# Scratch rows regrouped by their reader, and each unit's write cut in four

## The chip, the cores and the metric

The kernel runs on one core of one Trainium2 chip. The metric is the device time of one execution in microseconds (us), lower is better. On the core work TensorE (PE, matrix products), VectorE (DVE), ScalarE (ACT), GpSimd (POOL) and SyncE (SP, which only issues transfers here), and 16 DMA engines that carry all transfers between the on-chip buffers and DRAM. One execution is recorded by the hardware profiler; what it left is called the profile here (a page of summaries) and the trace (every instruction and transfer).

## The reference

The input `x` has 2048 rows of 1024 numbers. Two filters, A and B, are applied to it in the frequency domain and their results are mixed by a gate per row:

```python
x = A_x
g = sigmoid((x * gate_w).sum(-1, keepdims=True))
X = rfft2(x)                                   # 2048 x 513, complex
a = irfft2(X * (A_w_r + 1j * A_w_i), s=(S, D))
b = irfft2(X * (B_w_r + 1j * B_w_i), s=(S, D))
return g * a + (1 - g) * b
```

All inputs and the output are bfloat16; B's own `x` is not used.

## The kernel before, in words

The transforms are done as matrix products with constant matrices. The columns split into two halves, `par` 0 (even frequencies) and `par` 1 (odd). The work on rows goes forward in two steps (`f1`, 64 x 32), the columns are transformed in between, and the way back has the same two steps. Its tokens are:

- `r`, `f`, `E`, `O` (`f1`): the first step along rows, from `x` into the tile `Y`.
- `F` (`f2`, L375), `G` (`f3`, L394): per unit, the columns' transform and the second step along rows. There are 8 units (`u` = 0 to 7) per half; each has two tiles of 128 rows (`tt`).
- `c` (`cmul`, L415), with `d` (`edge`) and `a` (`part`): the product with the filter weights, on DVE; `w` (`load_w`, L232) loads the weights of a unit.
- `i` (`i1`, L453): the first step back. It runs twice per unit, `r` = 0 and 1 (real and imaginary part); its result is copied out of PSUM by ACT or DVE (L278, L280) into a buffer `rl` that holds, per partition, two tiles `tt`, two filters `a`, two parts `r` and 256 columns. After `r` = 1 the buffer is **written to a scratch tensor `sc` in DRAM** (L461).
- `q` (`fetch`, L470): **reads the scratch back**, with rows spread differently over the partitions. `q par.g.v` reads, for `v` of 8, what the four units of group `g` (units 0 to 3 or 4 to 7) wrote; it fills every second partition of a tile of 128 partitions with 4 KB each. So two fetches, g = 0 and g = 1, fill one tile.
- `j` (`i2`, L483): the second step back along rows, from such a tile, with the gate worked into its matrix `EAB`. `k` (`i3`, L498) and `D` (`i3d`, L532, L520): the transform of the columns back. `s` (`fold`, L551), `t` (`last`, L565 to L582): sums and differences, and the write of the output.

The scratch is there because the two steps back need different rows side by side on the partitions; the trip through DRAM does the exchange.

What sets the order is a list written out by hand, `ORDER`: one token after another is built, and each engine carries out its own instructions in that order. All loads, scratch writes, fetches and nearly all output writes are issued by SP, one after another; if one has to wait, everything behind it on SP waits. The writes stand in the list where their unit ends (`i0.1`, `i2.1`, `i1.1`, `i3.1`, `i4.1`, ... `i14.1`, `i15.1`); the half `par` 1 has units 8 to 15 in these tokens. Its first three fetches (`q1.0.1`, `q1.0.0`, `q1.0.2`) and then `q1.1.0` and the rest come behind `i15.1`. `j1.0` to `j1.7` read them.

Buffers are handed out by fixed lists (`SLOTS`). `rl` has 4 buffers, which the units of a half, and later the output, take in turn: a unit may write its buffer only when the transfers that read it before have landed. The transfers share 8 semaphores in turn, so that an issue also waits until the eighth transfer before it has landed.

The scratch is one tensor per half. Unit `u` writes, for each of its four (`tt`, `a`), 128 rows of 1 KB, one from each partition. Partition `p` is 32 k + s, with k from 0 to 3 and s from 0 to 31, and the fetch for `v` takes s from 4 v to 4 v + 3.

Of the kernel before, what the change touches and what calls it, by code (L numbers as in the profile page):

```python
# [10 lines left out]
P = 128  # L11
# [3 lines left out]
NU = 8  # L15
N1 = 32
N2 = 64
BF16 = mybir.dt.bfloat16
# [139 lines left out]
def gated_mix(ctx, tc, x_in, we_in, wo_in, gw_in, out):  # L158
    nc = tc.nc
# [18 lines left out]
    def take(tag, *dims):  # L178

        t = slots[tag][int(next(order[tag]))][:, 0:int(np.prod(dims))]  # L180
        ax = "abcd"[:len(dims)]
        return t.rearrange(f"p ({' '.join(ax)}) -> p {' '.join(ax)}", **dict(zip(ax, dims)))

    def halves():
        return [bank(), bank()]
# [18 lines left out]
    XR = [big.tile([P, 2064], BF16, name=f"xr{v}") for v in range(8)]  # L204
    RO = [big.tile([P, 2064], BF16, name=f"ro{v}") for v in range(8)]
# [7 lines left out]
    Ec = const.tile([P, N2], BF16, name="ec")  # L213
    Ez = const.tile([64, N2], BF16, name="ez")
    scratch = ctx.enter_context(tc.tile_pool(name="scratch", bufs=1, space=bass.MemoryType.DRAM))
    sc = [scratch.tile([NU, 4, P, 512], BF16, name=f"sc{par}") for par in range(2)]
    Y = big.tile([P, 2, 2, 2, 16, 2, 32, 2], BF16, name="y")
    y = [Y[:, par] for par in range(2)]
    wod = [big.tile([P, 2048], BF16, name=f"wo{k}") for k in range(4)]
# [56 lines left out]
    def evac(eng, out, in_):  # L276
        if eng == "A":
            nc.scalar.copy(out=out, in_=in_)  # L278
        else:
            nc.vector.tensor_copy(out=out, in_=in_)  # L280
# [6 lines left out]
    def hp(j):  # L287
        return slice(64 * j, 64 * j + 64)
# [153 lines left out]
    def i1(n, r, eng="A"):  # L442
        par, u = n // NU, n % NU
        p = Ps[n]
        o = 1 if par == 0 and r == 1 else 0
        ps = halves()
        terms = (((0, 0, 0), (2, 0, 1), (3, 1, 1), (2, 1, 0)), ((1, 0, 0), (0, 0, 1), (2, 1, 1), (0, 1, 0)))[r]
        terms = [z for z in terms if z[1:] not in summed.get(n, ())]
        for k, (w, q, a) in enumerate(terms):
            for tt in range(2):  # L450
                for j in range(2):
                    hin = hp(j ^ tt)
                    nc.tensor.matmul(ps[tt][hp(j), :], lhsT=WI[hin, 2 * u + tt, w, :],  # L453
                                     rhs=p[hin, q, tt, a::2, o:o + 256], start=(k == 0), stop=(k == len(terms) - 1))
        if r == 0:
            RLs[n] = take("rl", 2, 2, 2, 256)
        rl = RLs[n]
        for tt in range(2):
            evac(eng[tt % len(eng)], rl[:, tt, :, r, :], ps[tt][:].rearrange("p (a m) -> p a m", a=2))
        if r == 1:  # L460
            nc.sync.dma_start(sc[par][u].rearrange("t p f -> p t f"), rl[:].rearrange("p t a r m -> p (t a) (r m)"))  # L461
            RLs.pop(n), Ps.pop(n)

    def rows(par, v):
# [1 line left out]

    def fetch(par, g, v):

        src = sc[par][4 * g:4 * g + 4].rearrange("u t (k s) f -> (u t k) (s f)", k=4)
        nc.sync.dma_start((XR, RO)[par][v][g::2, 0:2048], src[:, 2048 * v:2048 * v + 2048])  # L470

    Vs, EVs = {}, {}
    IGU = FD[:, 0].rearrange("p a b m -> p (a b m)").rearrange("p (c a d) -> p c a d", c=2, a=2)
# [113 lines left out]
    def run(tok):  # L587
        op, a, e = tok[0], tok[1:].split(":")[0], tok.split(":")[1] if ":" in tok else ""
        n = [int(q) for q in a.split(".")] if a else []
        if op in "rfEO":  # L590
            f1(((n[0], 0), (n[0], 1)) if op in "rf" else ((n[0], "EO".index(op)), (n[0] + 1, "EO".index(op))), e)
        elif op in "VQ":
            xfold(n[0], op)
        elif op == "h":
            gt["z"] = gate_hat()
        elif op == "l":
            late()
        else:
            dict(F=f2, G=f3, d=edge, c=cmul, i=i1, w=load_w, g=gate_z, q=fetch, j=i2, k=i3, D=i3d,
                 s=fold, a=part, t=last)[op](*n, *([e] if e else []))  # L600
# [57 lines left out]
```

## Time and profile before

| | |
|---|---|
| time, three runs | 112.97, 118.17, 167.16 us (median 118.17) |
| the profiled execution | 113.11 us, of which the span of the profile is 111.3 us |
| busy, share of the span | PE 89%, ACT 84%, DVE 83%, POOL 7% |
| scratch writes | 16 of 512 KB, median 6.0 us from issue to landing |
| fetches | 32 of 256 KB, median 5.2 us (`par` 0) and 5.5 us (`par` 1) |
| DMA | 37.07 MB, mean 333 GB/s, 18,594 packets |
| granted TensorE clock | 1.00 |

How to read it: the span runs from the first to the last instruction. The busy time of an engine is the time in which it carries out instructions; matmuls are pipelined and their ends are modelled. A wait is counted for the engine that stands idle, under the name of what ended it. "SPq" is SP's sequence of transfers, where the listed duration is that of the issue, not of the transfer. Landing is the moment when a transfer's semaphore is complete. The lines that the argument rests on are shown where it is made.

### The profile page before, as it was taken

To read this page: it belongs to the slowest core of one execution; us is meant where nothing else is said; L and a number is where in the kernel's file an instruction comes from. 1 tells how busy PE (TensorE), PEld (TensorE's weight loads), DVE (VectorE), ACT (ScalarE), POOL (GpSimd) and SP (SyncE) were. 2 spreads that over 40 slices of the span, in tenths; PEclk is the share of its full clock that TensorE was granted. 3 is DMA by queue.
4 is the path that set the end of the run, shared out by engine and by line. 5 is a ranking of instruction groups with operands and counts; after the bars stand their busy time and mean duration, and the time that the engine had idled before them with its cause. 6 is when DMAs were issued, how large, how long until landed. Compare 5 with 4: busy or idle time off the path is not lost. (4 is left out here: it accounts for less than half of the span.)

```text
span 111.3 us, 4030 instructions
## 1 busy us (share of the span) xinstructions
PE 99.1 (89%) x1656; PEld 68.5 (62%) x1656; DVE 92.3 (83%) x145; ACT 94.0 (84%) x185; POOL 7.4 (7%) x14
## 2 busy tenths in 40 slices
PE   5959989799999999999999999995999775999740
PEld 2339979475556658656765677654699564664430
DVE  0169957399899999999999999995989869699770
ACT  2246977599899999999999999999799798999740
POOL 1000000121592000000000000000000000000000
PEclk9999999999999999999999999999999999999999
DMA  3899999999999998995999999999995789998974
GB/s 106 223 361 415 405 397 406 414 411 388 412 397 409 398 333 262 367 392 181 260 359 334 363 316 386 362 317 378 322 276 217 224 228 358 399 408 358 366 281 128
DMA packets 18594, 37.07 MB, mean 333 GB/s; under 512 B 2188, under 2 KB 11024, under 8 KB 18576
## 3 DMA queue, kind: packets, MB, share of 16 engines
q1 hardware_dynamic: 17696, 36.37, 90.5%
q10 hardware_dynamic: 848, 0.45, 1.4%
q8 instruction: 13, 0.21, 0.7%
q14 instruction: 5, 0.04, 0.1%
q0 software_dynamic: 32, 0.00, 0.0%
HBM read 24.23 MB, written 12.58 MB: 331 GB/s over the span
## 5 line engine op out<-in xcount | busy, mean ns | idle before, releaser
L453 PE MATMUL pt<-p,wi 64*64 64x512 bf16 x488 | 30.6, 377 | 0.0
L278 ACT CAST rl<-pt 128x512 bf16<-128x512 f32 x47 | 28.6, 920 | 0.7 <-PE pt L453 0.7
L415 DVE TENSOR_TENSOR p<-X,ro 128x4096 bf16<-128x4096 bf16 x11 | 25.1, 2293 | 0.4 <-ACT V L344 0.3
L278 ACT CAST T<-pt 128x512 bf16<-128x512 f32 (+1 forms) x40 | 23.2, 721 | 1.6 <-PE pt L532 0.6
L453 PEld LDWEIGHTS <-wi 64*64 64x64 bf16 x488 | 16.1, 106 | 9.6 <-issue 1.5
L278 ACT CAST X<-pt 128x512 bf16<-128x512 f32 x27 | 17.5, 824 | 0.9 <-PE pt L394 0.9
L278 ACT CAST V<-pt 128x512 bf16<-128x512 f32 x28 | 16.3, 690 | 1.6 <-PE pt L483 1.5
L278 ACT CAST y<-pt 128x512 bf16<-128x512 f32 x21 | 11.2, 627 | 5.6 <-PE pt L321 4.1
L375 PE MATMUL pt<-fd,y 128*128 128x256 bf16 x128 | 15.9, 273 | 0.0
L375 PEld LDWEIGHTS <-y 128*128 128x128 bf16 x128 | 11.6, 98 | 4.3 <-issue 2.9
L280 DVE CAST rl<-pt 128x512 bf16<-128x512 f32 x17 | 11.2, 677 | 0.1
L394 PE MATMUL pt<-T,wf 64*64 64x512 bf16 (+2 forms) x192 | 10.5, 307 | 0.6 <-issue 0.6
L498 PE MATMUL pt<-ig,V 128*128 128x256 bf16 x88 | 10.8, 273 | 0.0
L574 DVE TENSOR_TENSOR rl<-wo,T 128x1024 bf16<-128x1024 bf16 (+1 forms) x18 | 9.2, 569 | 1.6 <-ACT T L278 1.2
L498 PEld LDWEIGHTS <-V 128*128 128x128 bf16 x88 | 8.2, 98 | 1.5 <-issue 0.4
L415 DVE TENSOR_TENSOR p<-X,wo 128x4096 bf16<-128x4096 bf16 x4 | 9.1, 2274 | 0.0
L280 DVE CAST y<-pt 128x512 bf16<-128x512 f32 x11 | 7.4, 686 | 2.1 <-PE pt L324 2.0
L278 ACT CAST p<-pt 128x512 bf16<-128x512 f32 x15 | 8.5, 604 | 0.3 <-PE pt L498 0.2
L394 PEld LDWEIGHTS <-wf 64*64 64x64 bf16 x192 | 5.6, 107 | 3.3 <-issue 1.2
L369 POOL TENSOR_SCALAR ro<-ro 128x8 bf16<-128x8 bf16 x7 | 5.8, 850 | 22.6 <-DMA ro<-in_we_dram 22.6
L483 PE MATMUL pt<-eab,ro 128*128 128x64 bf16 x128 | 5.0, 193 | 2.6 <-DMA ro<-sc 1.9
L483 PEld LDWEIGHTS <-ro 128*128 128x128 bf16 x128 | 4.5, 98 | 3.8 <-issue 2.5
(57 smaller groups left out, 107.7 us busy)
## 6 DMA issues: line engine op xcount, KB each, us to landing
sc<-rl SPq DMA_DIRECT2D x16, 512.0 KB, 6.0
xr<-sc SPq DMA_DIRECT2D x16, 256.0 KB, 5.2
ro<-sc SPq DMA_DIRECT2D x16, 256.0 KB, 5.5
ro<-in_we_dram SPq DMA_DIRECT2D x7, 516.0 KB, 8.4
xr<-in_x_dram SPq DMA_DIRECT2D x6, 512.0 KB, 8.4
out_dram<-rl SPq DMA_DIRECT2D x5, 512.0 KB, 4.3
wo<-in_wo_dram SPq DMA_DIRECT2D x4, 512.0 KB, 7.8
ro<-in_wo_dram SPq DMA_DIRECT2D x4, 512.0 KB, 6.7
```

The source lines that it names most:

```text
L278: nc.scalar.copy(out=out, in_=in_)
L280: nc.vector.tensor_copy(out=out, in_=in_)
L369: nc.gpsimd.tensor_scalar(Ws[n][:, :, :, 257:258], Ws[n][:, :, :, 256:257], -1.0, None, ALU.mult)
L375: nc.tensor.matmul(ps[tt][:, e * 256:e * 256 + 256], lhsT=y[par][:, c, e, t].rearrange("p b s k -> p (b s k)"), rhs=FD[:, par, c, e, :], s ...
L394: nc.tensor.matmul(ps[tt][ho, dst:dst + ln], lhsT=WF[hp(j), 2 * u + tt, w, :], rhs=T[hp(j), tt, src:src + ln], start=(k == 0), stop=(k == 2))
L415: nc.vector.tensor_tensor(po, xo, wo, ALU.mult)
L453: nc.tensor.matmul(ps[tt][hp(j), :], lhsT=WI[hin, 2 * u + tt, w, :], rhs=p[hin, q, tt, a::2, o:o + 256], start=(k == 0), stop=(k == len(te ...
L483: nc.tensor.matmul(ps[s][:, ch * 128 + h * 64:ch * 128 + h * 64 + 64], lhsT=R[:, k, ch * 128:ch * 128 + 128], rhs=EAB[:, 4 * v + k, :], st ...
L498: nc.tensor.matmul(po, lhsT=V[:, s, 2 * r + c, :], rhs=IG[:, par, 2 * r + c, :], start=(c == 0), stop=(c == 1))
L574: nc.vector.tensor_tensor(o4[:, k, h] if not isinstance(od, list) else o4[:, k.start, h], x, y_, op)
```

## The change

The scratch tensor of a half, which had the dimensions unit, four (`tt`, `a`) rows, partition, 512 numbers, gets the dimensions group, 32 quarters of the partitions, 16 (unit of the group, `tt`, `a`), 4 partitions, 512 numbers. The four partitions that one fetch reads together still lie side by side (4 KB), and now the 16 such pieces of a group's units do as well (64 KB); before, they lay 128 KB apart. [...] The fetch reads the same rows into the same partitions in the same order.

```diff
-    sc = [scratch.tile([NU, 4, P, 512], BF16, name=f"sc{par}") for par in range(2)]
+    sc = [scratch.tile([2, 32, 16, 4, 512], BF16, name=f"sc{par}") for par in range(2)]
@@ i1
         if r == 1:
-            nc.sync.dma_start(sc[par][u].rearrange("t p f -> p t f"), rl[:].rearrange("p t a r m -> p (t a) (r m)"))
+            for tt in range(2):
+                for a in range(2):
+                    nc.sync.dma_start(sc[par][u // 4, :, 4 * (u % 4) + 2 * tt + a], rl[:, tt, a].rearrange("p r m -> p (r m)"))
             RLs.pop(n), Ps.pop(n)
@@ fetch
-        src = sc[par][4 * g:4 * g + 4].rearrange("u t (k s) f -> (u t k) (s f)", k=4)
-        nc.sync.dma_start((XR, RO)[par][v][g::2, 0:2048], src[:, 2048 * v:2048 * v + 2048])
+        src = sc[par][g].rearrange("(k v) t s f -> t k v (s f)", k=4)
+        nc.sync.dma_start((XR, RO)[par][v][g::2, 0:2048], src[:, :, v])
```

## The prediction

> **What bounds the kernel now.** I read busy time by stretches first, since a share over the whole span mixes stages. Columns: stretch, length, busy time of PE, PE's weight loads, DVE, ACT, POOL (instructions in brackets), granted clock, busy share of the DMA engines, GB/s.
>
> ```profile
> 68.00:72.00 4.00, 3.99 (x80) 2.79 (x76) 4.00 (x5) 4.00 (x11) 0.00 (x0) 1.00 1.07 376
> 72.00:76.00 4.00, 3.02 (x62) 1.84 (x53) 3.97 (x4) 4.00 (x10) 0.00 (x0) 1.00 1.00 334
> 76.00:80.00 4.00, 3.67 (x56) 2.51 (x57) 2.67 (x4) 3.21 (x7) 0.00 (x0) 1.00 1.06 374
> 80.00:84.00 4.00, 4.00 (x86) 3.78 (x84) 3.56 (x9) 4.00 (x9) 0.00 (x0) 1.00 0.85 259
> 84.00:88.00 4.00, 3.81 (x47) 3.21 (x45) 3.66 (x7) 3.74 (x8) 0.00 (x0) 1.00 0.61 196
> 88.00:92.00 4.00, 2.81 (x48) 2.49 (x48) 2.98 (x7) 3.07 (x7) 0.00 (x0) 1.00 0.85 245
> 92.00:96.00 4.00, 2.79 (x55) 2.00 (x54) 3.97 (x9) 3.47 (x8) 0.00 (x0) 1.00 0.98 368
> ```
>
> From 30 to 72 us ACT and DVE are full: nothing done to the scratch pays there. From 72 on they have holes. ACT idles 0.79 + 0.26 + 0.93 + 0.53 us in the rows above and 0.74 in 100 to 104: **3.25 us is the most that faster scratch traffic can return**. The waits of 72 to 108 us (engine and line, for what, us in total, times, longest) say whose holes they are:
>
> ```profile
> PE pt L483 <- DMA ro<-sc: 1.9, 3, 0.6
> ...
> PEld L483 <- DMA xr<-sc: 1.4, 1, 1.4
> ```
>
> L483 is `i2`, the reader of the fetches. Fetch by fetch: q1.1.1 lands at 89.78 and j1.1 starts at 89.82, q1.1.2 92.66 and 92.69, q1.0.6 99.30 and 99.32. So the second half's fetches pace the kernel from 88 to 99 us, and they are paced by three things. One: they may only start when i15.1's write has landed (issued 80.16, landed 85.34; SP waits 2.6 us for it, below). Two: SP issues one per 0.64 us. Three: stalls. Undisturbed fetches land 0.63 us apart (92.03, 92.66, 93.27, 93.91, 94.55), 416 GB/s; three gaps are longer (1.36, 2.26, 1.14 us), 0.72 + 1.61 + 0.50 = 2.8 us of stall in all. The packet records agree: a 4 KB packet takes 159 ns, in this stretch up to 1,833.
>
> Then SP's own waits, 50 to 72 us, whole, and the first of 72 to 96:
>
> ```profile
> SPq L470 <- DMA sc<-rl: 3.6, 2, 2.4
> SPq L461 <- ACT rl L278: 2.1, 4, 1.0
> SPq L461 <- ACT T L278: 1.6, 2, 1.2
> SPq L461 <- ACT X L278: 1.4, 1, 1.4
> SPq L256 <- PE pt L453: 1.2, 1, 1.2
> SPq L470 <- PE pt L453: 0.5, 1, 0.5
> ...
> SPq L461 <- DVE rl L280: 4.4, 2, 3.7
> SPq L470 <- DMA sc<-rl: 2.6, 1, 2.6
> SPq L461 <- ACT rl L278: 2.2, 3, 1.5
> ```
>
> The first six add to 10.4 us; 2.4 of them end at 50.3, so in 50.3 to 72 SP has **8.0 us to spare**. This is what the change spends.
>
> **The change, part by part.** (a) *48 more issues on SP*, three for each of 16 units. Their price is the unknown that decides. The rows for issues, with min/median/max ns:
>
> ```profile
> L470 SPq DMA_DIRECT2D ro<-sc x8: 594/596/599, 85.9 to 90.4; - x8
> ...
> L208 SPq DMA_DIRECT2D xr<-in_x_dram x5: 389/424/432, 0.7 to 2.6; - x5
> ...
> L461 SPq DMA_DIRECT2D sc<-rl x5: 359/360/366, 72.0 to 80.2; - x5
> ```
>
> An issue after a pause costs 0.36; back to back, a load of 128 rows costs 0.43 and a fetch of 64 rows 0.60, each plus 0.04 between. That the fetch's 0.594 to 0.599 doesn't move while landings stall says that it is the issue's own cost. The one other transfer of 64 rows, `ez`, took 0.52 where loads of 128 rows took 0.33. So the ends for a second write are 0.48 and 0.70 us (the fetch's 0.64 and some for one more dimension). The new write has 128 rows in the buffer and 32 in DRAM; a side with fewer than 128 rows is what sets the dear rows apart, so I take the fetch's **0.64**. A unit then holds SP for 0.42 + 3 x 0.64 = 2.34 us instead of 0.42.
>
> Before 50 us SP mostly waits for data (its next write is issued up to 4 us after the last), and the engines are full: free, as long as no weight load queued behind a write becomes late; the nearest, w14, has some 15 us. In 50.3 to 72 six units are written: 18 x 0.64 = 11.5 us against 8.0, so SP reaches i12.1 at 75.5 instead of 72.0. Then i12, i11, i13 and i14 take 4 x 2.34 = 9.4, to 84.9; their data was ready by 76, so the waits of this stretch are all eaten. i15.1's fourth issue comes at 84.9 + 0.42 + 1.28 = 86.6.
>
> (b) *Landing.* The old write lands 5.2 to 6.5 us after its issue, behind queued data. Paced by issues, 128 KB per 0.64 us is 205 GB/s, half of what the engines move, so the queue drains; a 128 KB output at the end lands 1.9 us after its issue, a 256 KB one 2.2. I take 2.2: the last piece lands at 88.8 instead of 85.34. The fetch q1.1.0 now waits for sixteen pieces instead of four transfers; behind it on SP stand the other fetches and then all output writes, and `i2` on PE waits for them: 13 fetches start **3.5 us late**. Eight transfers are in flight at most (each issue waits for the semaphore of the eighth before it); with small pieces that is 1 MB, 5.1 us of issues, so it binds only where landings take longer than that.
>
> The Trainium skill, "DMA: Bandwidth & Descriptors", section "Issuing engines are not separate DMA queues", holds that the time to start a transfer is usually small beside the transfer. Here 128 KB at 416 GB/s is 0.31 us, under any issue in the trace; by the page's rule part (a) would cost nothing and the faster rival below would follow.
>
> (c) *The `rl` buffers.* A unit's buffer comes free when all its writes have landed, and it is close already: i8's write lands at 71.33 and i13.0 is evacuated into the same buffer from 71.41; i10's 73.12 and i14.0 73.32; i12's 78.53 and i15.0 78.70. Later issues with quicker landings leave these between 0 and 1.5 us later; where they come later, ACT and PE stop. I count 0, since this lies ahead of, and beside, the lateness of (b), and keep 1.5 for the range.
>
> (d) *Fetches.* Same number, bytes and 4 KB runs; sixteen neighbouring pieces of 4 KB are read together where each group of four rows lay 128 KB from the next. Bounds for the stalls: none of 2.8 us goes, or all. The writes get a wide pitch in turn (two 4 KB runs per engine, engines 128 KB apart), so I take half: 1.4. The issue may cost 0.05 more with one dimension more; over 13 fetches 0.6, kept for the range.
>
> (e) *First half's fetches.* j0.2 waits for q0.1.2 (issued 71.12, landed 76.28). 3.5 us late in issue, 2 us quicker in landing: 1.5 us late, and it is part of the same lateness, as i15.0 stands behind j0.2 on PE.
>
> **Sum.** The first late fetch is 3.5 late, the last 3.5 - 1.4 = 2.1. ACT has 0.93 + 0.53 + 0.74 = 2.2 us of holes behind 88 us; late work fills some of them, but j1.6 starts at its fetch's landing and has 9 us of work behind it. So the end moves by 2.1 to 3.5 less what is filled: I take +2.6. On the profiled execution's 113.11 us (span 111.3 and 1.8 around it) this is **115.7 us**. The three runs shown are 112.97, 118.17 and 167.16, median 118.17; the profile belongs to the lowest, and I forecast beside that one.
>
> **Rivals.**
> *Cheap issues and no stalls: faster.* At 0.48, 18 x 0.48 = 8.6 exceeds the 8.0 by 0.6; four units of 1.86 end at 80.0, i15.1 is on time, its last issue is at 81.5 and lands at 83.7, 1.6 us earlier than now; with the 2.8 us of stalls gone, fetches run 4 us ahead and ACT's holes bound the gain: 1.6 to 3.2, say 110.7. It decides at an issue of about 0.52. For it: loads of 128 rows; against it: every transfer with 64 rows.
> *The pieces collide: much slower.* At 0.70, SP is 4.6 late at i12.1; 4 x 2.52 = 10.1; last landing near 90.7, 5.4 late; no stall goes, since now the writes stride; less 1 us filled: 117.5. With (c) added, 119.
> *No relief in the fetches, issues between.* At 0.55, 9.9 - 8.0 = 1.9 late; four of 2.07 from 73.9 end at 82.2, the last piece lands at 85.9, 0.6 late; stalls stay: 113.7, no change. The trace knows stalls without scratch: the x loads' 4 KB packets near 4 us took up to 1,353 ns. The Trainium skill's same page, "Latency and other measured facts", gives a row pitch of 512 KiB 207 of 214 GB/s, so a quarter of that pitch should cost almost nothing and the layout gains almost nothing; the fetches' gaps here (2.8 us on some 8) are more than that rule allows.
> *It doesn't do what it says.* If the interleaved writes were taken as overlapping, each would wait for the one before, over 2 us each, 64 times: above 200 us. Fetches g=0 and g=1 into alternate partitions of one buffer don't wait for each other now, so I give it 0.03.
>
> **Chances.** Forecast 0.40 (its times 114.3 to 117, four fifths of them over 2%), much slower 0.18, no relief 0.17, faster 0.22, wrong ordering 0.03. Slower by over 2% (about what a measurement here tells from no change), above 115.4: 0.32 + 0.18 + 0.03 = 0.53. Within 2%: 0.08 + 0.17 + 0.03 of the faster case = 0.28. Faster: 0.19. The range takes in the faster rival's 110.7 and the much slower one's 119: 110.5 to 119.
>
> **What would show it.** Write issues behind a unit's first: 0.60 right, under 0.45 wrong. SP's waits for ACT and DVE between 50 and 80 us nearly gone. i15.1's last piece landing near 88.8. Stretch 88 to 92 emptier on ACT than 3.07. Fetch landings evenly 0.64 apart if the layout helps. I am wrong if issues are cheap, or if SP's lateness is absorbed because the queue's backlog, not SP, set the landings.

## The result, and the profile after

The changed kernel takes 129.33 us (median; 127.28 to 129.91), the kernel before in the same measurement 115.66 (112.97 to 167.16): **slower, ratio 1.133, 95% interval 1.101 to 1.166**. The ratios here and below leave disturbed runs out, so they can differ from the quotient of the medians; for e5 to e9 only medians are given, and the traces of e8, e10, e12 and e14 are of disturbed runs. The forecast was 115.7 with a range of 110.5 to 119: the sign was right, the size was far off. The profiled execution took 127.28 us (before 113.11), of which the span is 125.2 (111.3).

The page of the changed kernel: span, busy time by engine, PE's and the granted clock's rows of slices of 3.1 us, and the issues of scratch writes and second-half fetches (count, size, median us to landing).

```profile
span 125.2 us, 4122 instructions
...
PE 102.9 (82%) x1656; PEld 69.6 (56%) x1656; DVE 92.5 (74%) x145; ACT 94.4 (75%) x185; POOL 7.1 (6%) x14
...
PE   6969897999999999999992599509999079959750
...
PEclk9999999999999999999999679985999968999999
...
sc<-rl SPq DMA_DIRECT2D x64, 128.0 KB, 3.6
...
ro<-sc SPq DMA_DIRECT2D x16, 256.0 KB, 6.0
```

PE was busy 99.1 us before and idle for 12.2 (111.3 less 99.1). Now it is idle for 22.3 (125.2 less 102.9): 10.1 us more waiting. The other 3.8 us are the same matmuls at a lower granted clock. Together that is the 13.9 us. PE's row has three holes ahead of its end (digits 2, 0 and 0), and behind each the clock's row drops. Stretch by stretch, with the columns of the table in the prediction:

```profile
66.00:70.00 4.00, 0.56 (x6) 0.25 (x3) 2.55 (x2) 2.07 (x5) 0.00 (x0) 1.00 0.94 270
70.00:74.00 4.00, 3.61 (x52) 2.28 (x56) 0.69 (x1) 1.74 (x4) 0.00 (x0) 0.57 0.96 303
74.00:78.00 4.00, 4.00 (x84) 2.14 (x80) 3.59 (x3) 4.00 (x9) 0.00 (x0) 1.00 0.72 227
78.00:82.00 4.00, 2.07 (x44) 1.07 (x36) 3.31 (x4) 3.36 (x7) 0.00 (x0) 1.00 1.05 267
82.00:86.00 4.00, 1.80 (x21) 1.55 (x22) 0.69 (x1) 0.59 (x1) 0.00 (x0) 0.72 0.84 275
```

In the first row PE stands for 3.4 of 4 us; in the second it works at a clock of 0.57. The full engines of 68 to 72 us before (3.99, 4.00 and 4.00 on PE, DVE and ACT) are gone. What PE waited for, from the waits of 30 to 126 us (engine and line, for what, us in total, times, longest; `i2` is L485 now, the fetch L472, the write L463):

```profile
PE pt L485 <- DMA ro<-sc: 5.5, 3, 3.8
...
PE pt L485 <- DMA xr<-sc: 4.1, 1, 4.1
...
PE pt L485 <- DMA sc<-rl: 3.8, 1, 3.8
...
DVE rl L280 <- DMA sc<-rl: 0.3, 1, 0.3
```

The three long ones are one fetch each. q0.1.0 lands at 70.26 (before 65.23) and j0.0 starts at 70.29; q0.1.2 lands at 84.16 (76.28), j0.2 starts at 84.20; q1.1.0 lands at 100.67 (88.42), j1.0 starts at 100.70. The release of the first carries the name of a scratch write because that came last by the profile, but j0.0's start goes with its fetch's landing. The fourth line is all that the `rl` buffers cost here by being held for scratch writes: 0.3 us.

From the landing of q1.1.0 to the end of the span the kernel takes 24.5 us (125.2 less 100.67), before 22.9 (111.3 less 88.42). So 12.2 of the 13.9 us are the lateness of this one landing, and what has to be explained is why it is so late.

Why the fetches are late is in SP's own sequence (start, length, what, count), of before and then of after:

```profile
72.00 8.53 SPq L461 DMA_DIRECT2D sc<-rl  x5
80.62 13.93 SPq L470 DMA_DIRECT2D ro<-sc  x16
```

```profile
75.77 3.14 SPq L472 DMA_DIRECT2D xr<-sc  x5
79.01 15.32 SPq L463 DMA_DIRECT2D sc<-rl  x20
94.37 10.84 SPq L472 DMA_DIRECT2D ro<-sc  x16
```

SP reaches i12.1 at 79.01 instead of 72.00 (forecast 75.5), and the twenty writes of the last five units hold it until 94.33. i15.1's last piece is issued at 93.73 and lands at 95.86 (forecast 86.6 and 88.8; before 80.16 and 85.34). The price of a write was forecast well. The issue rows of after (min/median/max ns), the writes and the fetches, from 60 and 96 us on:

```profile
L463 SPq DMA_DIRECT2D sc<-rl x34: 518/594/2102, 60.1 to 93.7; - x34
...
L472 SPq DMA_DIRECT2D ro<-sc x11: 514/593/595, 96.4 to 102.7; - x11
```

0.594 and 0.04 between: the 0.64 that was taken. But the first write of a unit costs it too (0.52 to 0.60, where 0.36 was read off the old write), so a unit holds SP for 2.55 us, not 2.34.

SP's sequence can be summed up. From i5.1's first write at 51.2 us to i15.1's last stand 44 writes, 15 fetches and a load, 60 issues. At 0.64 us from one start to the next, the last would start at **88.9 if SP never waited again** (51.17 + 59 x 0.64). The forecast's 86.6 was such a sum without waits too, with 0.42 us for the first write of each of the eleven units; the right price of these adds 2.3 us. Another 4.8 us came on the way to 93.73. The profile lists 6.2 us of waits for SP in 50 to 97 us, and these lead:

```profile
SPq L463 <- ACT rl L278: 1.8, 4, 0.5
SPq L463 <- ACT T L278: 1.0, 2, 0.5
SPq L463 <- ACT X L278: 0.7, 2, 0.6
```

They are short (0.6 us at most), and most of them end inside the issue that carries them: i7.1's first write, listed with a wait of 0.5 us, takes 0.556 us, and a piece without a wait 0.60. So they hardly lengthen the sequence, and SP's waits were nearly all eaten, as forecast. What lengthens it are five issues of 0.85 to 2.10 us (at 51.75, 58.87, 72.86, 79.62 and 90.94), 3.6 us beyond 0.60 each, and about 1.2 us of gaps for data and for landings; the other 55 issues take 0.51 to 0.62 us. For four of the five the profile names no wait. In the trace each of the five overlaps a load of 16 KB of instructions (packets of queue q8, from 51.33, 58.59, 72.47, 79.59 and 91.01 us; the last took 1.6 us, the issue beside it 2.1). In e3 the five longest issues of this stretch (at 51.79, 59.29, 72.54, 81.18 and 92.62) overlap such loads as well. That the loads make the issues long is suggested by this and not shown; in the kernel before, one of 1.14 us (at 56.87) has neither a wait nor a load beside it.

### The profile page after: what moved, and what is told of

It reads as the page before. It is cut to its first block, busy times and chain, and to the rows that moved or that the text cites. A ratio compares the mean times of both kernels' runs of the same rounds, so it can differ in the third digit from the quotient of the medians.

```text
span 125.2 us, 4122 instructions
## 1 busy us (share of the span) xinstructions
PE 102.9 (82%) x1656; PEld 69.6 (56%) x1656; DVE 92.5 (74%) x145; ACT 94.4 (75%) x185; POOL 7.1 (6%) x14
## 5 line engine op out<-in xcount | busy, mean ns | idle before, releaser
L278 ACT CAST rl<-pt 128x512 bf16<-128x512 f32 x47 | 27.3, 778 | 2.1 <-PE pt L453 2.1
L278 ACT CAST V<-pt 128x512 bf16<-128x512 f32 x28 | 15.0, 618 | 11.8 <-PE pt L485 11.8
L453 PEld LDWEIGHTS <-wi 64*64 64x64 bf16 x488 | 15.2, 108 | 10.9 <-issue 2.4
L278 ACT CAST X<-pt 128x512 bf16<-128x512 f32 x27 | 16.0, 763 | 1.6 <-PE pt L394 1.6
L500 PE MATMUL pt<-ig,V 128*128 128x256 bf16 x88 | 12.4, 299 | 0.0
L485 PE MATMUL pt<-eab,xr 128*128 128x64 bf16 x128 | 5.5, 205 | 8.0 <-DMA xr<-sc 4.1
L485 PE MATMUL pt<-eab,ro 128*128 128x64 bf16 x128 | 5.7, 205 | 5.5 <-DMA ro<-sc 5.5
L500 PEld LDWEIGHTS <-V 128*128 128x128 bf16 x88 | 9.0, 107 | 2.2 <-issue 0.4
L485 PEld LDWEIGHTS <-xr 128*128 128x128 bf16 x128 | 5.0, 105 | 8.8 <-DMA xr<-sc 4.3
L485 PEld LDWEIGHTS <-ro 128*128 128x128 bf16 x128 | 5.1, 106 | 6.8 <-issue 6.0
```

What stands on the lines that cost most here:

```text
L485: nc.tensor.matmul(ps[s][:, ch * 128 + h * 64:ch * 128 + h * 64 + 64], lhsT=R[:, k, ch * 128:ch * 128 + 128], rhs=EAB[:, 4 * v + k, :], st ...
L500: nc.tensor.matmul(po, lhsT=V[:, s, 2 * r + c, :], rhs=IG[:, par, 2 * r + c, :], start=(c == 0), stop=(c == 1))
```

## The experiments

### Which part costs: the cut, the layout or the read

**e1** cuts the write in four and leaves layout and fetch as they were. A piece has 128 rows on both sides.

```diff
-            nc.sync.dma_start(sc[par][u].rearrange("t p f -> p t f"), rl[:].rearrange("p t a r m -> p (t a) (r m)"))
+            for tt in range(2):
+                for a in range(2):
+                    nc.sync.dma_start(sc[par][u, 2 * tt + a], rl[:, tt, a].rearrange("p r m -> p (r m)"))
```

> The old scratch layout with four writes of 128 KB per unit, each 128 rows on both sides; fetches as before. If the 32-row side of the new write is what makes its issue dear (0.55 to 0.60 us in the changed kernel), the issues here cost 0.33 to 0.45, a unit holds SP for about 1.8 us, and the kernel is within 2 us of before (113 to 115). If any issue behind another costs 0.60, a unit holds SP for 2.5 us, the last write is issued near 89 to 91 us and the kernel takes 118 to 122. Fetches should land 0.63 to 0.64 us apart in both cases, 4 KB packets at 159 ns.

**e2** keeps the one old write and gives the fetch the changed kernel's list: 16 pieces of 4 KB for each of 4 k.

```diff
-        src = sc[par][4 * g:4 * g + 4].rearrange("u t (k s) f -> (u t k) (s f)", k=4)
-        nc.sync.dma_start((XR, RO)[par][v][g::2, 0:2048], src[:, 2048 * v:2048 * v + 2048])
+        src = sc[par][4 * g:4 * g + 4].rearrange("u t p f -> (u t p f)").rearrange("(k v t e) -> t k v e", k=4, v=8, t=16)
+        nc.sync.dma_start((XR, RO)[par][v][g::2, 0:2048], src[:, :, v])
```

> One write of 512 KB per unit in the old layout, but the fetches read the addresses that the changed kernel reads (16 neighbouring pieces of 4 KB, four times, 512 KB apart). So the fetched rows are not the ones that the transform needs; the work and its order are the same. If the new read pattern itself is slow, 4 KB packets take about 254 ns here too, fetches of the second half land 1.0 us apart, and 13 of them cost 4.8 us more: 116 to 119. If the slow fetches come from what the small writes left behind (their place in DRAM, or their order), packets are at 159 ns and the kernel takes 111 to 114.

**e3** is the reverse: the changed kernel's layout and four writes, and a fetch of a list of 64 pieces, 32 KB apart.

```diff
-        src = sc[par][g].rearrange("(k v) t s f -> t k v (s f)", k=4)
-        nc.sync.dma_start((XR, RO)[par][v][g::2, 0:2048], src[:, :, v])
+        src = sc[par][g].rearrange("q t s f -> (q t s f)").rearrange("(w e) -> w e", w=64)
+        nc.sync.dma_start((XR, RO)[par][v][g::2, 0:2048], src[:, 2048 * v:2048 * v + 2048])
```

> The four writes of the changed kernel, with its layout, but fetches that read 64 rows of 4 KB, 32 KB apart, as before (so not the rows that the transform needs). If issue cost on SP is the larger part of the loss, this has the changed kernel's lateness of the writes (issues 0.55 to 0.60, last write near 88 to 92 us) and fetches 0.64 us apart: 118 to 123. If the read pattern is nearly all of the loss, it is 113 to 116.

**e4** is the kernel before with blocks padded by four rows, so that a pitch of 132 KB takes the place of 128 KB. The padded source can't be one list of 64, so its fetch is a list of 16 by 4.

```diff
-    sc = [scratch.tile([NU, 4, P, 512], BF16, name=f"sc{par}") for par in range(2)]
+    sc = [scratch.tile([NU, 4, P + 4, 512], BF16, name=f"sc{par}") for par in range(2)]
...
-        src = sc[par][4 * g:4 * g + 4].rearrange("u t (k s) f -> (u t k) (s f)", k=4)
-        nc.sync.dma_start((XR, RO)[par][v][g::2, 0:2048], src[:, 2048 * v:2048 * v + 2048])
+        src = sc[par][4 * g:4 * g + 4, :, 0:P].rearrange("u t (k s) f -> (u t) k (s f)", k=4)
+        nc.sync.dma_start((XR, RO)[par][v][g::2, 0:2048], src[:, :, 2048 * v:2048 * v + 2048])
```

> Before, with each of a unit's four blocks of 128 rows padded by four rows, so that the 16 groups of a fetch lie 132 KB apart instead of 128 KB; one write per unit, all results as before. If the stalls of the fetches of before came from the pitch of 128 KB, the long gaps between landings (2.8 us in the second half) go and the kernel gains 1 to 3 us: 110 to 112.5. If they have another cause, it is within 1% of before. If the shape of the access (16 by 4 rows instead of 64) is what made the changed kernel's fetches slow, packets take about 254 ns here and the kernel takes 116 to 119.

Measured beside the kernel before (113.67 us, 110.62 to 117.58): e1 119.44, ratio 1.074 (1.060 to 1.087); e2 113.17, 1.022 (1.000 to 1.044); **e3 126.33, 1.135 (1.122 to 1.149)**; e4 112.76, 1.014 (1.004 to 1.025). The four writes in the new layout are the whole loss (1.135 beside the change's 1.133), with a list for the read as before. Of it, a bit over half comes from there being four (7.4 of 13.5%), the rest from the shape of each. A slow read by itself costs 2.2% in e2, with an interval that begins at 1.000, and 1.4% in e4; in the changed kernel it adds nothing that shows. Against what was expected, e1's issues are as cheap as its first theory says and its time is that of its second; e3 is slower than both of its theories; e2's packets are slow (204 ns) and its time is not; and e4 gains nothing, though its long gaps go. The stretch of SP with the last twenty writes, and the issue rows, in e1 and then in e3:

```profile
75.95 12.04 SPq L463 DMA_DIRECT2D sc<-rl  x20
```

```profile
L463 SPq DMA_DIRECT2D sc<-rl x32: 319/431/1319, 64.0 to 87.5; - x32
```

```profile
80.58 14.23 SPq L463 DMA_DIRECT2D sc<-rl  x20
```

```profile
L463 SPq DMA_DIRECT2D sc<-rl x36: 518/597/1538, 59.3 to 94.2; - x36
```

Both issue 128 KB. With 128 rows on both sides the issue costs 0.431 us, with 32 rows in DRAM 0.597. SP reaches i12.1 4.6 us later in e3 and needs 2.2 more for the last twenty writes: 6.8 of the 7.0 us between the spans (117.5 and 124.5). So the dear issue comes with the 32-row side, as argued, and its price acts nearly one for one on the end. But e1 refutes the schedule of the faster rival: at 0.43 + 0.05, under the 0.52 from which it should have won, i15.1's last write is issued at 87.54 and lands at 90.56, not at 81.5 and 83.7, and the kernel is 7% slower. The rival's other condition, fetches without stalls, is not met in e1; but the 2.8 us that it counted for them are less than half of what e1 loses (7.4%, some 8 us).

### How many more issues SP can take

**e7** cuts the old write in two of 256 KB, 16 more issues in place of 48.

```diff
-            nc.sync.dma_start(sc[par][u].rearrange("t p f -> p t f"), rl[:].rearrange("p t a r m -> p (t a) (r m)"))
+            for tt in range(2):
+                nc.sync.dma_start(sc[par][u, 2 * tt:2 * tt + 2].rearrange("t p f -> p t f"), rl[:, tt].rearrange("p a r m -> p a (r m)"))
```

> The old layout with two writes of 256 KB per unit, 128 rows on both sides. If the loss of the four writes (7.4%, 8 us) is SP time over a reserve of 8 us between 50 and 72 us, one more issue of 0.48 us for each of six units (2.9 us) stays inside the reserve and the time is that of before, 111 to 115. If each issue costs in proportion, a third of the loss is there: 116.

**e8** has e1's four writes in the second half only (`if par == 1`), and the one old write in the first.

```diff
-            nc.sync.dma_start(sc[par][u].rearrange("t p f -> p t f"), rl[:].rearrange("p t a r m -> p (t a) (r m)"))
+            if par == 1:
+                for tt in range(2):
+                    for a in range(2):
+                        nc.sync.dma_start(sc[par][u, 2 * tt + a], rl[:, tt, a].rearrange("p r m -> p (r m)"))
+            else:
+                nc.sync.dma_start(sc[par][u].rearrange("t p f -> p t f"), rl[:].rearrange("p t a r m -> p (t a) (r m)"))
```

> The old layout; one write per unit in the first half of the columns, four (128 rows each) in the second half, so that SP's extra issues begin at 62 us. If the loss of the four writes builds up from 50 us on, because fetches of the first half stand behind late writes, stop PE and so delay the last units too, then leaving out units 0 to 7 brings back more than half of it: 112 to 116. If only the last units' writes count, it stays at 118 to 120.

**e6** is the changed kernel with the two writes of tile 0 issued by POOL.

```diff
-                    nc.sync.dma_start(sc[par][u // 4, :, 4 * (u % 4) + 2 * tt + a], rl[:, tt, a].rearrange("p r m -> p (r m)"))
+                    (nc.gpsimd if tt == 0 else nc.sync).dma_start(sc[par][u // 4, :, 4 * (u % 4) + 2 * tt + a], rl[:, tt, a].rearrange("p r m -> p (r m)"))
```

> The changed kernel, with the writes of tile 0 of each unit issued by POOL, which is idle then, and those of tile 1 by SP. If SP's issue time is what costs (a unit holds SP for 2.6 us), it holds SP for 1.25 us here and most of the 14 us comes back: 113 to 118. If the small strided writes cost in the DMA engines or in their landing, it stays at 123 to 130. POOL's own issues may take about 1 us each; if they limit, a unit's first pieces come late and it stays above 120 with SP waiting.

Beside the kernel before (113.9 us, 111.86 to 117.44): e7 114.32 (112.58 to 118.94), e8 117.55 (116.55 to 118.47), e6 118.74 (117.16 to 119.31). SP's last writes in e7 and in e6:

```profile
72.08 8.70 SPq L462 DMA_DIRECT2D sc<-rl  x10
```

```profile
74.03 9.60 SPq L463 DMA_DIRECT2D sc<-rl  x10
```

e7 reaches i12.1 at 72.08, as before (72.00), and takes 8.70 us for ten writes as before for five (8.53). SP's waits do hold 16 more issues, at no cost that shows. In e6 the pieces, their layout and their sizes are the changed kernel's, and half of them are issued by POOL: SP has 5 us back at i12.1, and by the medians about 9 of the change's 14 us come back (4.8 us of loss are left). POOL's half also goes in other packets (4 KB instead of 1 KB) and has semaphores of its own. But the pieces land no sooner for it (median 5.0 us for POOL's and 5.1 for SP's, where the changed kernel's take 3.6), and the changed kernel hardly waits for the semaphores (0.6 us in 50 to 97 us). With e1 and e3, where the price of an issue sets the loss, this shows SP's time for issues to be the main cause, and not what the pieces do in the DMA engines. e8 missed what was expected: leaving the first half's writes whole returns only somewhat over a third of e1's loss (3.7 us of loss by the medians, where e1 has 5.8). The lateness at i15.1 is made by the units of the second half as well: its last write lands at 89.22, in e1 at 90.56, before at 85.34.

### Issues alone

**e9** is the kernel before with three idle transfers of 2 KB behind each unit's write, on SP. Nothing of the scratch is cut.

```diff
+    dum = scratch.tile([48, 32, 8, 8], BF16, name="dum")
...
+            for m in range(3):
+                nc.sync.dma_start(dum[3 * n + m, :, 0:4, :], F1[:, 0:8])
```

> The kernel before, with three more transfers behind each unit's write, of 2 KB each (128 rows of 16 bytes, 32 by 4 in DRAM, to a place that nobody reads): the issues of the changed kernel without its layout, without its cut data and with no fetch that waits for them. Each adds about 0.6 us on SP, 1.9 us per unit. If SP's time alone makes the loss, the kernel takes 122 to 127, like the run with the four small writes and the old fetches (126.3), with PE's two waits of about 4 us at L483 near 66 to 72 and 80 to 86. If the loss needs the cut or strided writes themselves (landing, DRAM), it stays below 117.

It takes 135.83 us (134.01 to 138.46) beside 114.52, more than either theory gave. Issues with hardly any data cost this much with all that they set off, so the run is no clean measure of the issue alone. From its waits of 50 to 124 us:

```profile
ACT rl L279 <- DMA sc<-rl: 11.4, 5, 3.6
DVE rl L281 <- DMA sc<-rl: 10.9, 3, 4.0
```

Here the `rl` buffers come free late. The idle transfers take turns with the scratch writes at the eight semaphores, so SP also stands still for the landing of scratch writes (3.8 and 1.9 us in its waits). The changed kernel has little of that (0.6 us for landings in its waits of 50 to 97 us).

### One late fetch, or SP throughout

Two of the three PE stops are fetches of the first half, and q0.1.2 stands late in the list though j0.2 is early to need it. **e11** is the kernel before with q0.1.2 and q0.1.5 exchanged, **e12** the changed kernel, **e13** e1 and **e14** e6 with the same exchange.

```diff
-q0.0.0 i6.1:AV c9 i7.1:AA F11:VA F12:AV c10 l g1 q0.0.5 i9.0:AA q0.0.6 q0.0.3 q0.1.5 i8.0:VA q0.1.0 G11:AA G12:AA c11
+q0.0.0 i6.1:AV c9 i7.1:AA F11:VA F12:AV c10 l g1 q0.0.5 i9.0:AA q0.0.6 q0.0.3 q0.1.2 i8.0:VA q0.1.0 G11:AA G12:AA c11
...
-G14:VA i12.0:AA q0.1.1 G15:VA q0.1.4 q0.1.6 q0.1.2 i12.1:AA i13.0:AA i11.1:AA c14 c15 i13.1:AA i14.0:VA a15.1:V
+G14:VA i12.0:AA q0.1.1 G15:VA q0.1.4 q0.1.6 q0.1.5 i12.1:AA i13.0:AA i11.1:AA c14 c15 i13.1:AA i14.0:VA a15.1:V
```

> The kernel before, with the places of two fetches exchanged in the order: q0.1.2, which j0.2 waits for at 75 to 76 us, is issued near 60 us and q0.1.5, which is needed at 81, near 71. If fetches of the first half cost PE time through their place on SP, the wait of 1.4 us goes and the kernel gains 0.5 to 1 us; if something else ends that wait at the same time, it stays the same within 0.3 us.

> The changed kernel with the places of q0.1.2 and q0.1.5 exchanged in the order, so that the fetch that PE waits 4.1 us for at 80 to 84 us (q0.1.2, issued at 78.3) is issued near 65 instead. If the late fetches of the first half feed back (PE stands still, units 11 to 15 come later, and so do their writes), that wait goes, i15.1's last piece is issued 2 us or more earlier and the kernel takes 123 to 126. If SP's time for the issues alone sets the end, its last write still comes near 93 us and the kernel stays at 126.5 to 130.

> Four writes of 128 KB in the old layout, with the fetches q0.1.2 and q0.1.5 exchanged in the order. Without the exchange PE stood 3.9 us for q0.1.2 (76.2 to 80.1), the granted clock was 0.59 and 0.56 in the two stretches of 4 us after it, and the ratio was 1.074. Theory (one late fetch is the loss): the 3.9 us wait is gone or under 1, the granted clock stays near 1.00 in 78 to 86, i15.1's last write is issued before 84 instead of 87.5, time 112 to 115 us. Rival (SP's issues set the end whatever the fetch does): another wait of 3 to 7 us takes its place further on, as in the changed kernel with the same exchange, and the time stays at 118 to 120.

> The changed kernel with half of each unit's writes issued by POOL, and q0.1.2 and q0.1.5 exchanged. Without the exchange 118.7 us, with a 2.0 us PE wait for q0.1.2 and a 2.2 us one for q0.1.0. Theory (the rest is first-half fetches come late): the 2.0 us wait goes and 2 to 3 us come back, 115 to 117. Rival (the rest is the slow landings and fetches of the second half): no change, 118 to 119.5.

| | without the exchange | with it | ratio of the latter to the kernel before |
|---|---|---|---|
| kernel before | 114.52 | e11: 112.31 | 0.986 (0.976 to 0.995) |
| changed kernel | 129.33 | e12: 128.04 | 1.139 (1.119 to 1.158) |
| e1 | 119.44 | e13: 120.6 | 1.070 (1.057 to 1.083) |
| e6 | 118.74 | e14: 115.38 | 1.013 (1.001 to 1.026) |

e12, PE's and ACT's waits of 50 to 107 us, and SP's last writes:

```profile
PE pt L485 <- DMA ro<-sc: 6.8, 1, 6.8
...
PE pt L485 <- DMA xr<-sc: 4.1, 1, 4.1
ACT rl L278 <- DMA sc<-rl: 4.0, 2, 3.1
```

```profile
80.54 14.64 SPq L463 DMA_DIRECT2D sc<-rl  x20
```

The stop at j0.2 is gone, but SP ends its writes at 95.2, no earlier than without the exchange (94.3), and the gained time is waited at j1.0 (6.8 us, where it was 3.8) and for `rl` buffers (4.0). So the PE stop at j0.2 is a symptom, and SP's sequence sets the end. e13 missed: the one late fetch, and the lower clock behind it, looked like e1's whole loss, and without it the time is the same. From its waits of 50 to 112 us, SP's own waits of 50 to 97, and SP's sequence:

```profile
ACT rl L278 <- DMA sc<-rl: 4.0, 1, 4.0
```

```profile
SPq L463 <- DMA xr<-sc: 2.9, 6, 1.0
```

```profile
76.68 12.53 SPq L463 DMA_DIRECT2D sc<-rl  x20
```

SP is at i12.1 at 76.68, 4.7 us late, so i12's buffer lands late and ACT stands 4.0 us for it, where the fetch stood before. Two fifths of SP's waits of 50 to 97 us (2.9 of 7.1 us in all) are now for the landing of the eighth transfer before: eight issues of 0.48 are 3.8 us, and a fetch in e1 takes 4.8 us to land (median). This limit was set aside in the prediction for 5.1 us of issues, and at the cheaper issue it binds for part of the time. How much of e1's 7% it makes was not separated.

e14 did as its theory said: by the medians 3.4 us come back, and the changed kernel stands 1.3% behind the kernel before once SP has half of the writes and one fetch comes earlier. e11, the exchange alone, is 1.4% faster than the kernel before, the only ratio here below 1: PE's wait of 1.4 us for `xr` in the prediction's table falls to 0.4. Beside e11, which has the same exchange, the changed kernel in e14 is some 2.7% behind (1.013 over 0.986, from two measurements).

### Why reads in the new shape are no faster

**e5** has the one old write and a fetch of a list of 64 pieces that lie 8 KB apart. In the kernel before, the list of 64 has an even pitch of 32 KB: pieces of one k lie 128 KB apart, and those of the other three k lie between them.

```diff
-        src = sc[par][4 * g:4 * g + 4].rearrange("u t (k s) f -> (u t k) (s f)", k=4)
-        nc.sync.dma_start((XR, RO)[par][v][g::2, 0:2048], src[:, 2048 * v:2048 * v + 2048])
+        src = sc[par][4 * g:4 * g + 4].rearrange("u t p f -> (u t p f)").rearrange("(c w h e) -> c h w e", c=4, w=64, h=2)[v // 2, v % 2]
+        nc.sync.dma_start((XR, RO)[par][v][g::2, 0:2048], src)
```

> One write of 512 KB per unit as before; the fetches read 64 rows of 4 KB that lie 8 KB apart (not the rows that the transform needs), as one list of 64 as before, not as 16 by 4. If the nearness of the rows is what slowed packets (median 204 ns with the changed kernel's addresses and one write per unit), packets take over 200 ns here and landings are 0.8 to 1.0 us apart. If the 16 by 4 shape is what slowed them (it also gave a median of 209 ns with the addresses of before and 4 KB of padding), packets take 159 ns and landings are 0.64 apart, and the long gaps are gone or not, which tells whether the pitch of 128 KB made those. Time 111 to 114 in both cases.

112.66 us (111.58 to 113.23) beside 113.9. Fetches at full stretch, in e2 (16 by 4, near), e4 (16 by 4, pitch 132 KB) and e5 (64, near); the last column is GB/s:

```profile
88.00:92.00 4.00, 3.53 (x64) 2.91 (x64) 3.30 (x7) 3.46 (x8) 0.00 (x0) 1.00 1.02 293
```

```profile
88.00:92.00 4.00, 3.56 (x64) 2.87 (x64) 2.90 (x6) 3.22 (x7) 0.00 (x0) 1.00 1.01 313
```

```profile
92.00:96.00 4.00, 3.20 (x57) 2.21 (x56) 3.97 (x10) 3.98 (x10) 0.00 (x0) 1.00 0.99 381
```

All three keep the DMA engines full, but move 293, 313 and 381 GB/s. In the second half's fetches a 4 KB packet takes 159 ns (median) in every kernel whose fetch is a list of 64, near (e5) or far (e1, e3, before), and 204 to 255 ns in every one whose list is 16 by 4, near (the changed kernel, e2, e12) or far (e4). So nearness bought nothing and the list's shape costs. In exchange the long gaps nearly vanish with it (fetches of e4 land 0.84 us apart, of e2 0.9 with one gap of 1.55, of the changed kernel 1.0 with one of 2.53), while in e5 they stay (1.12, 1.52 and 1.48) though the pieces are 8 KB apart. The wide pitch is therefore not what makes the stalls; what does, and why the shape matters, stays open.

### POOL as the issuer

**e10** is the kernel before with its one write per unit issued by POOL.

```diff
-            nc.sync.dma_start(sc[par][u].rearrange("t p f -> p t f"), rl[:].rearrange("p t a r m -> p (t a) (r m)"))
+            nc.gpsimd.dma_start(sc[par][u].rearrange("t p f -> p t f"), rl[:].rearrange("p t a r m -> p (t a) (r m)"))
```

> The kernel before, with each unit's one write issued by POOL. SP then never waits for a unit's data ahead of a fetch. If SP's order (fetches behind writes that wait for ACT and DVE, 8 us in 50 to 72) costs in the kernel before, fetches of the first half come some us earlier and PE's wait of 1.4 us at 75 us goes: 1 to 2 us less. If the fetches are bound by the transfers ahead of them in the DMA engines or by the writes' landing, it is within 1%; POOL's slower start of a transfer, about 1 us for the one that it issues now, may cost 1 us at the last unit.

119.32 us beside 114.52, ratio 1.053 (1.045 to 1.061). SP is free of all writes, and it is slower, which neither theory had. POOL's issue takes 0.75 us, its transfers go in packets of 4 KB instead of 1 KB, and a write took up to 10 us to land (68.1 to 78.3). SP's fetches wait for these landings (27.0 us in 50 to 97 us), and the DMA share falls to 0.45 in 60 to 64 us and to 0.14 in 88 to 92. POOL itself waits for the data (24.1 us for ACT's copies into `rl`). The cause of the slow landings was not found.

## Why the prediction missed, step by step

- **What bounds the kernel before**: that nothing done to the scratch pays before 72 us is contradicted by no run, in the sense that nothing was gained there. That nothing could be lost there did not follow: two of the three stops are first-half fetches.
- **(a), price of an issue**: right, 0.594 + 0.04. The choice by the 64-row fetch rather than the 128-row load is shown by e1 against e3. The *first* write at 0.42 was mis-sized: it is a piece like the others and takes 0.64 with the gap, which for eleven units makes 2.3 us. By the rule of the Trainium skill cited there ("DMA: Bandwidth & Descriptors", section "Issuing engines are not separate DMA queues") the issues would have cost next to nothing; the runs disagree, since e1 loses 7.4% by cutting the same bytes into 48 more issues.
- **(a), SP's sequence: the step that failed.** i15.1's fourth issue was put at 86.6 and came at 93.73, 7.1 us later. The 8.0 us to spare were spent nearly as forecast; about 1.2 us of waits stayed where the forecast had them "all eaten". The sum that they were set against was too small: 2.3 us are the first writes, and 3.6 us are issues that take long by themselves, for which the forecast had nothing. So SP was 7.0 us late at i12.1 and not 3.5, and the last five units took 15.3 us where the forecast had 11.7 (5 x 2.34) and twenty issues at 0.64 make 12.8. What makes single issues long stays open. e7 shows that the reserve does hold 16 issues, e1 that it does not hold 48 even at 0.48: forecast 0.6 us late at i12.1, measured 3.95.
- **(b), landing**: 2.13 us for the last piece where 2.2 was taken (the row of 2.2 us is that of a 128 KB output from SP; the one of 256 KB took 2.3). 13 fetches late was right in kind; the last write's landing is 10.5 us late (95.86 less 85.34) and not 3.5, and the first fetch behind it lands 12.2 us late.
- **(c), the `rl` buffers at 0**: 0.3 us in the changed kernel. e12 and e13 show that the wait (4.0 us each on ACT) is next in line where the stop at j0.2 is gone.
- **(d), half of the stalls gone**: the sign was wrong. The long gaps went but for one of 2.53 us, yet in the second half fetches land about 1.0 us apart instead of 0.63, as the 4 KB packets take about 250 ns instead of 159. The last fetch lands 14.1 us later than before (113.41 less 99.30), where 2.1 were forecast. This is not what made the end late: in e3 the last fetch lands at 110.87, 2.5 us earlier than in the changed kernel, and the span is only 0.7 us shorter. The extra dimension costs the issue nothing (0.593).
- **(e), first half's fetches 1.5 us late**: mis-sized. q0.1.2 is 7.9 us late, q0.1.0, which the forecast didn't name, 5.0.
- **What was left out**: PE's clock. PE's busy time grew by 3.8 us. Behind each of the three stops the clock is at 0.50 for over 3 us (70.1 to 73.5, 83.8 to 87.1 and 100.9 to 104.2).
- **The rivals.** Faster: refuted by e1. Much slower: nearest with 119, but it got there by an issue of 0.70, where the price was 0.64 and SP's sequence was longer than summed up. No relief: the pitch is indeed not what makes the stalls (e5), but the price of the issues overrode it. False ordering: did not occur, the writes are issued 0.64 us apart.

## What to carry over

Sum up the issuing engine's own sequence from the point where it is last idle for long to the issue that the end waits for: so many issues at so many us, the first of each group at the price of the others, with some room for issues that take 1 to 2 us without a wait that the profile names. If that sum comes near the time available, each cut of a transfer costs its issue on the path. Cut a transfer only if the engine that issues it has room at that very place in its order, and look at what shape the pieces get: for the same 128 KB an issue cost 0.43 us here with 128 rows on both sides and 0.60 with 32 rows in DRAM.

## What the runs showed of the hardware that was not expected

- A PE stop costs more than its length. In the changed kernel stops of 3.8 to 4.1 us were each followed by over 3 us at a granted clock of 0.50. The Trainium skill, "TensorE: Matmul & The Clock Gate", section "Part 1: The HAM clock gate", puts the fall to half speed behind an idle window of about 3.4 us; these three agree. But in e13 stops of 2.6 and 2.1 us too were followed by stretches of 2 us at 0.50, while one of 2.0 us in e6 and three of 2.9 to 3.3 us in e9 were not.
- A read of 64 pieces of 4 KB, with the DMA engines full, moves 381 GB/s as one list of 64 (e5), and 293 to 313 as a list of 16 by 4 with the same bytes (e2, e4).
- 512 KB writes issued by POOL made the kernel 5% slower although POOL waited only for the data (e10).
